# Writing out the order of attention half by half, in a kernel that runs block-sparse attention beside a two-layer product

## The chip, the core and the metric

One core of a Trainium2 chip runs the whole program. Its engines have a queue each and take their instructions in order: TensorE (PE, with its weight loads as PEld), VectorE (DVE), ScalarE (ACT), GpSimd (POOL), and SyncE (SP), which here only starts transfers. The metric is the time of one execution on the device, in microseconds.

## What is computed

Block-sparse attention over 4 batches, 8 heads, 768 positions and 64 elements a head. Positions are cut into 24 blocks of 32. A query block sees its neighbours, the first and the last block, and three sampled blocks; the first and the last query block see everything. Then two products with an exact Gelu between.

```python
mask = np.abs(blk_i - blk_j) <= window            # window = 1
mask = mask | (blk_i == 0) | (blk_j == 0) | (blk_i == n_blocks - 1) | (blk_j == n_blocks - 1)
for qb in range(n_blocks):
    for kb in sampled_blocks[qb]:                 # 3 of 24
        mask[qb * block:(qb + 1) * block, kb * block:(kb + 1) * block] = True
scores = np.where(mask, scale * q @ k.T, -1e9)
attn = softmax(scores) @ v                        # (4, 8, 768, 64)
...
x = attn.transpose(0, 2, 1, 3).reshape(3072, 512)
h = x @ w_in                                      # 512 -> 2048
g = 0.5 * h * (1.0 + erf(h / sqrt(2)))
out = g @ w_out                                   # 2048 -> 512
```

## The kernel before

**Units and stages.** The work is cut into eight units: half a batch each, 384 positions, three tiles ("quads") of 128. Units 0, 2, 4, 6 are the dense halves: they hold the two end blocks too, which see all 24 blocks. Units 1, 3, 5, 7 hold inner blocks alone. The loop at line 728 goes over units; in step n it issues the first products of unit n (`ffn1_step`, 64 matmuls, Gelu on ACT), and then the second products of unit n as 48 "pieces" (`ffn2_pieces`, one matmul each, 16 to an output tile), mixed into the attention of unit n+1. The pieces keep PE at work while DVE and ACT do the softmax. The first attention (unit 0) has idle products in their place, and the last second products stand alone (`last_output`).

**Rounds and groups.** A dense unit has four dense rounds `("d", x, G)`: one end block x (first or last) with one half G of the heads. All units have sparse rounds `("s", blocks)` of one or two query blocks; two sparse rounds, or one group of three blocks, make a group of up to 128 rows. In order, a round goes through `scores` (PE), `maxima` (DVE), `exponentials` (ACT) and `turned` (a transpose on DVE); a group goes through `values` (PE, in two halves), `divided` (DVE), and `outputs` (PE transposes, then an ACT copy into `xT`, which the next first products read). Where a unit of inner blocks is followed by a dense one, two rounds of the latter are done ahead (`ahead`).

**Buffers.** Scores take one of two buffers of `psA`, which is free again when the round's exponentials are done, and which the first products use as well. Values use `psV` (the last group of some units `psA`). Two banks change roles (`roles`): one holds the output tile of the pieces, the other takes the transposes of `outputs` and of `turn_pair`; they swap as a new output tile begins. So an output tile that is finished must be copied out by `store` (an ACT copy, line 532, then a transfer by SP) before the next transposes can use its bank. `ffn2_pieces` puts a finished tile in the list `finished`, and `store_finished` issues its copy wherever it is called: at the start of each new tile, and in `attention`.

**Order.** Nothing reorders the program: it stands in each engine's queue as the Python code issues it. Before, `attention` runs a loop over rounds. Each turn issues the scores of the next round, a division, a transpose, the maxima, the exponentials, a number of pieces from the list `quota`, an output, and value halves when `due`. `hooks` and `behind` put other work at given turns.

**Stage 0** has most of that: the keys and queries of batch 1 are turned on PE there, pair by pair (`turn_pair`, k0 to k3 and q0 to q3), each into the free bank and from there by a copy on ACT or DVE. `later_values` makes POOL read one element of turned query pair 2 (`hold_loads`), and then starts the eight loads of batch 1's values. In stage 1, DVE copies blocks into `gb` for unit 2 (`gather`, 27 copies on line 305), which read these values; unit 2's first `maxima` stands behind them in DVE's queue.

Of the kernel before, what the change touches and what calls it, by code (L numbers as in the profile page):

```python
# [10 lines left out]
F32 = mybir.dt.float32  # L11
# [9 lines left out]
def kernel(  # L21
# [10 lines left out]
    nc = tc.nc  # L32
# [213 lines left out]
    def turn_pair(which, pr):  # L246

        pt = turning_bank([P, PI, PP], "pt")
        turn_heads(which, pr, pt)
        dve = pr == 1  # L250
        if which == "k":
            (nc.vector.tensor_scalar_mul if dve else nc.scalar.mul)(
                keys(1)[:, 0:NB, BL * pr:BL * pr + BL].rearrange("q n (a i) -> q n a i", i=PI),
                pt.rearrange("q i (n a) -> q n a i", n=NB), 1.0 / 8.0)
        else:
            (nc.vector.tensor_copy if dve else nc.scalar.copy)(
                qTs[1][:, :, pr, :].rearrange("q c (p i) -> q c p i", i=PI),
                pt.rearrange("q i (c p) -> q c p i", c=NC))
# [50 lines left out]
    class Unit:  # L309
        def __init__(self, b, quads, dense):  # L310
            self.b, self.quads, self.dense = b, quads, dense
            self.groups = [[j for j in range(4 * t, 4 * t + 4) if 0 < j < NB - 1] for t in quads]
            self.js = [j for grp in self.groups for j in grp]
            self.place = {j: i for i, j in enumerate(sorted(self.js))}
            if b == 0 and dense:

                self.place = {j: 6 * t + i for t, grp in enumerate(self.groups) for i, j in enumerate(grp)}
            self.rounds = [("d", x, G) for G in (0, 1) for x in (0, 1)] if dense else []
# [15 lines left out]

    st = {}

    def scores(unit, rnd):
        qT, kT = qTs[unit.b % 2], keys(unit.b) if unit is not units[0] else k0
        A = psA.tile([P, 1024], F32, name="sc", tag="A")

        def product(o, G, hh, j, rhs):
            r = (hh % 2) ^ G
            rows = slice(64 * r, 64 * r + 64)
            pr = 2 * G + hh // 2
            nc.tensor.matmul(o, lhsT=qT[rows, j // 4, pr, BL * (j % 4):BL * (j % 4) + BL],  # L345
                             rhs=rhs(rows, pr), start=True, stop=True)
        if rnd[0] == "s":
            A4 = A.rearrange("p (g j c) -> p g j c", g=2, j=2)
            for i, j in enumerate(rnd[1]):
                x = unit.place[j]  # L350
                for hh in range(4):
                    for G in range(2):
                        product(A4[32 * hh:32 * hh + 32, G, i, :].rearrange(
                            "p (a c k) -> p a c k", a=2, k=BL), G, hh, j,
                            lambda rows, pr: seen_keys(x, rows, pr))
        else:
            _, x, G = rnd
# [4 lines left out]
        st[rnd, "A"] = A  # L362

    def maxima(rnd):
        A = st[rnd, "A"]
# [216 lines left out]
    def attention(unit, filler, quota, tail, hooks=None, late=False, ahead=None, when=None, behind={}):  # L582

        early = unit in closing
        done = begun.pop(unit, 0)  # L590
        rounds = [(unit, rnd) for rnd in unit.rounds[done:]]
        due = [(e - done + 1 + half, grp, half) for e, grp in sorted(unit.ends.items()) for half in range(2)]
        if when:
            due = [(at,) + x[1:] for at, x in zip(when, due, strict=True)]
# [3 lines left out]
        n, hooks = len(rounds), hooks or {}  # L598
        weighed, given = [], []

        def fill(m):
            for _ in range(m):
                next(filler, None)

        def weigh(it):
            _, grp, half = due.pop(0)
            halves = (half,)
            if due and due[0][0] <= it and due[0][1] == grp:
                halves += due.pop(0)[2:]
            values(unit, grp, halves)  # L610
            if 1 in halves:
                weighed.append(grp)

        def divide():
            divided(weighed[0])
            given.append(weighed.pop(0))
        for it in range(-1, n):
            last = it + 1 == n
            if not last:
                scores(*rounds[it + 1])  # L620
            else:
                while due and due[0][0] <= it:
                    weigh(it)
            ready = len(given)
            if weighed and not last:
                divide()
            if weighed and last and not early:
                divide()
            if it >= 1:
                turned(rounds[it - 1][1])  # L630
            if not last:
                maxima(rounds[it + 1][1])
            if it >= 0:
                exponentials(rounds[it][1])
            if last and not ahead:
                table(AF.Gelu)
            store_finished()
            for f in hooks.get(it, ()):
                f()
            fill(quota[it + 1])  # L640
            if not late:
                store_finished()
            if ready:
                outputs(unit, given.pop(0))
            while not last and due and due[0][0] <= it:
                weigh(it)
            for f in behind.get(it, ()):
                f()
        turned(rounds[n - 1][1])
        if early:  # L650
            divide()
        for f in hooks.get(n, ()):
            f()
        for m in tail[:-2]:
            fill(m)
            weigh(-1)
        assert not due
        fill(tail[-2])
        while len(given) > (not weighed):
            outputs(unit, given.pop(0))  # L660
        if weighed:
            divide()
        fill(tail[-1])
        outputs(unit, given.pop(0), 2)
        if ahead:
            table(AF.Gelu)
        for _ in filler:
            pass
        store_finished()
# [48 lines left out]
    attention(units[0], idle_products(30), [0, 3, 1, 8, 3, 6, 1, 1, 1, 2, 0], (0, 0, 0, 4),  # L718
              when=(5, 6, 7, 7, 8, 8, 10, 11),
              hooks={0: [lambda: fixed(1)], 1: [lambda: fixed(2, nc.scalar.copy, 0)],  # L720
                     3: [lambda: fixed(2, nc.scalar.copy, 1)], 4: [values_of(0)],
                     6: [values_of(1)], 8: [values_of(2)], 10: [more_numbers(J1[:3])]})

    def next_keys(b):
        place_keys(b)
# [2 lines left out]
    for n, unit in enumerate(units):  # L728
# [41 lines left out]
        if nxt is None:  # L770
            last_output(n)
        elif fresh:
            attention(nxt, filler, [1, 9, 4, 4, 4, 5, 3, 8, 3], (0, 0, 1, 4),
                      when=(2, 3, 4, 5, 6, 6, 8, 9))
        elif b + 1 < B:
            quota, tail, hooks, behind = [3, 10, 5, 4, 3, 8, 1, 5, 1], (0, 6), {}, {}
            if n == 0:
                quota, tail = [3, 11, 2, 3, 3, 6, 3, 4, 2], (0, 5)

                def later_values():  # L780
                    hold_loads(qTs[1][0:1, 0, 2, 0:1])
                    load_values(1)

                def pair(which, pr, pieces=0):
                    return [partial(next, filler, None)] * pieces + [partial(turn_pair, which, pr)]
                hooks = {1: pair("k", 0), 2: pair("k", 1, 2), 3: pair("q", 0, 1), 4: pair("k", 2, 2),
                         5: [later_values], 6: pair("q", 3), 8: [partial(spare_key, keys(1))]}
                behind = {3: pair("q", 1), 4: pair("q", 2), 5: pair("k", 3)}
            attention(nxt, filler, quota, tail, ahead=units[n + 2], hooks=hooks, behind=behind)
        else:  # L790
            attention(nxt, filler, [5, 8, 5, 5, 3, 8, 4], (0, 0, 1, 5),
                      when=(2, 3, 4, 4, 6, 7))


# [28 lines left out]
```

## Time and profile before

| what | us |
|---|---|
| median of three runs (lowest, highest) | 281.38 (281.14, 282.98) |
| the profiled execution | 284.88 |
| its span, first to last instruction | 283.1 |
| PE busy in the span | 253.0 |
| DVE, ACT, POOL busy | 206.3, 207.7, 101.7 |
| opening and unit 0's attention, to the first of the first products | 41.7 |
| last second products and the end | 13.7 |

A row of the order of time gives start, length, engine and line, operation, what it writes and reads with its size, how often it came in a row, and in brackets the idle time of the engine before it with what ended that. Waits on buffers show there. The mean granted clock of TensorE was 0.986.

### The profile page before, as it was taken

What the parts mean: (1) busy time and instruction counts of PE and PEld (TensorE: products, weight loads), DVE (VectorE), ACT (ScalarE), POOL (GpSimd) and SP (SyncE); (2) the same over time, 40 slices, a digit from 0 to 9 for tenths busy, and PEclk for the clock granted to TensorE, in tenths of its full rate; (3) what the DMA queues carried; (4) which work ended last, traced back from release to release, by engine and by line L of the source; (5) the groups of instructions that cost most, each with busy time, mean ns of one, the idle gap of its engine ahead of it and who ended that gap; (6) DMA issues with size and microseconds to landing.
All of it is one profiled execution on the core that took longest, in us unless ns stands there. A gap on an engine that the chain in (4) does not pass through costs nothing.

```text
span 283.1 us, 11427 instructions
## 1 busy us (share of the span) xinstructions
PE 253.0 (89%) x4860; PEld 143.6 (51%) x4918; DVE 206.3 (73%) x475; ACT 207.7 (73%) x380; POOL 101.7 (36%) x209
## 2 busy tenths in 40 slices
PE   1787669999898989999999899999999999999995
PEld 1623445455554455545564555445544566356644
DVE  7599839386779998688998878698948988782000
ACT  8779825896777885699668876896778866995611
POOL 8788950701897000580595000930040005000000
PEclk9999959999999999999999999999999999999999
DMA  6997299931999512991399218991101020021002
GB/s 101 175 89 124 40 195 202 206 73 40 95 156 145 132 41 73 122 99 51 23 153 171 71 42 132 95 75 43 41 0 39 8 76 0 0 80 39 2 37 75
DMA packets 72981, 23.80 MB, mean 84 GB/s; under 512 B 63073, under 2 KB 69474, under 8 KB 72930
## 3 DMA queue, kind: packets, MB, share of 16 engines
q0 software_dynamic: 56912, 13.64, 81.5%
q1 hardware_dynamic: 16018, 9.44, 12.9%
q8 instruction: 38, 0.62, 0.9%
q14 instruction: 13, 0.11, 0.1%
HBM read 27.26 MB, written 6.29 MB: 119 GB/s over the span
## 4 chain that ended last, share of the span: by engine, by line
PE 70%; DVE 12%; issue 6%; ACT 5%; DMA 4%; POOL 1%; DVEq 0%; POOLq 0%; ACTq 0%
PE hp L522 26%; PE op L548 20%; PE av L468 9%; PE sc L345 5%; DMA qn<-in_q_dram 4%; DVE nm L370 4%; DVE pT L404 2%; PE tx L497 2%; ACT pp L387 2%; PE op L578 2%; PE av L431 2%; DVE gb L305 2%; DVE nm L373 2%; PE pt L234 1%; PE av L578 1%
## 5 line engine op out<-in xcount | busy, mean ns | idle before, releaser
L522 PE MATMUL hp<-xT,w_in_sb 128*128 128x384 bf16 x512 | 85.1, 328 | 0.6 <-ACT xT L505 0.6
L387 ACT ACTIVATE pp<-sc,nm 128x256 bf16<-128x256 f32 x176 | 75.1, 544 | 9.4 <-DVE nm L370 9.1
L548 PE MATMUL op<-w_out_sb,g 128*128 128x512 bf16 x285 | 73.3, 380 | 6.3 <-issue 6.0
L522 PEld LDWEIGHTS <-w_in_sb 128*128 128x128 bf16 x512 | 50.3, 98 | 35.6 <-issue 3.0
L527 ACT ACTIVATE g<-hp 128x768 bf16<-128x768 f32 x56 | 45.2, 809 | 27.3 <-PE hp L522 27.3
L370 DVE TENSOR_REDUCE nm<-sc 128x4 f32<-128x1024 f32 (+1 forms) x48 | 52.8, 1106 | 7.9 <-PE sc L345 7.8
L305 POOL COPY gb<-kv 128x388 bf16 (+1 forms) x87 | 36.6, 474 | 24.8 <-DVE gb L296 22.9
L548 PEld LDWEIGHTS <-g 128*128 128x128 bf16 x336 | 27.7, 98 | 34.6 <-issue 10.4
L305 DVE COPY gb<-kv 128x388 bf16 x177 | 39.4, 300 | 1.9 <-DMA qn<-in_q_dram 1.9
L404 DVE STREAM_TRANSPOSE pT<-pp 128x512 f32<-128x512 f32 (+1 forms) x48 | 31.5, 656 | 6.6 <-ACT pp L387 6.4
L468 PEld LDWEIGHTS <-pT 64*32 64x32 bf16 (+1 forms) x2400 | 26.5, 92 | 18.0 <-issue 6.8
L468 PE MATMUL av<-kv,pT 64*32 64x130 bf16 (+1 forms) x1344 | 29.7, 223 | 3.9 <-issue 2.4
L165 POOL COPY mark<-gb 1x1 bf16<-1x1 bf16 x6 | 1.1, 179 | 79.7 <-DVE gb L305 79.7
L505 ACT COPY xT<-tx 128x512 bf16<-128x512 bf16 (+1 forms) x32 | 13.5, 448 | 13.7 <-PE tx L497 13.7
L141 POOL DMA_DIRECT2D kv<-in_v_dram x32 | 22.8, 721 | 1.8 <-DMA qn<-in_q_dram 1.1
L345 PE MATMUL sc<-gb,qT 64*32 64x256 bf16 x704 | 19.3, 274 | 3.6 <-ACT pp L391 1.5
L391 ACT ACTIVATE pp<-sc,nm 128x768 bf16<-128x768 f32 x16 | 17.2, 1107 | 5.9 <-DVE nm L373 5.9
L468 PE MATMUL av<-gb,pT 64*32 64x130 bf16 x1056 | 20.0, 224 | 0.0
L345 PEld LDWEIGHTS <-qT 64*32 64x32 bf16 x832 | 10.2, 90 | 19.1 <-issue 15.1
L415 ACT ACT_TABLE_LOAD x15 | 19.2, 1283 | 0.2
L487 DVE TENSOR_TENSOR xh<-av,rec 128x512 bf16<-128x512 f32 (+2 forms) x28 | 18.2, 652 | 1.0
L373 DVE TENSOR_REDUCE nm<-sc 128x1 f32<-128x768 f32 x16 | 14.7, 940 | 5.2 <-PE sc L345 4.9
(79 smaller groups left out, 232.8 us busy)
## 6 DMA issues: line engine op xcount, KB each, us to landing
out_dram<-os SPq DMA_DIRECT2D x23, 256.0 KB, 2.4
kv<-in_v_dram POOLq DMA_DIRECT2D x32, 96.0 KB, 6.6
w_out_sb<-in_moe_w_out_dram POOLq DMA_DIRECT2D x2, 1024.0 KB, 13.4
kn<-in_k_dram POOLq DMA_DIRECT2D x4, 384.0 KB, 11.3
qn<-in_q_dram POOLq DMA_DIRECT2D x4, 384.0 KB, 12.8
qn<-in_q_dram POOLq DMA_DIRECT2D x12, 128.0 KB, 5.4
kn<-in_k_dram POOLq DMA_DIRECT2D x12, 128.0 KB, 5.4
w_in_sb<-in_moe_w_in_dram POOLq DMA_DIRECT2D x2, 512.0 KB, 9.8
```

What stands on the lines that cost most here:

```text
L141: nc.gpsimd.dma_start(out=kvs[b % 2][32 * hh:32 * hh + 32, 0:NB, c0:c0 + D], in_=v[b, h].rearrange("(n p) d -> p n d", p=BL))
L305: (engine or nc.vector).tensor_copy(sampled(unit.place[j], r)[:, None, c0:c1], src[:, bass.ds(at[j][r], 1), :])
L345: nc.tensor.matmul(o, lhsT=qT[rows, j // 4, pr, BL * (j % 4):BL * (j % 4) + BL], rhs=rhs(rows, pr), start=True, stop=True)
L370: nc.vector.tensor_reduce(out=nm[:, 0:2 * n].rearrange("p (g j) -> p g j", g=2), in_=A4[:, :, 0:n, :], op=ALU.max, axis=AX.X, negate=True)
L373: nc.vector.tensor_reduce(out=nm[:, 0:1], in_=A[:, 0:S], op=ALU.max, axis=AX.X, negate=True)
L387: nc.scalar.activation(at[:, x // n, x % n], A[:, a:a + 256].rearrange("p (e c k) -> p e c k", e=2, k=BL), AF.Exp, bias=nm[:, x:x + 1])
L404: nc.vector.transpose(pt.rearrange("p g c x -> p (g c) x")[:, :, 64 * s:64 * (s + n)].bitcast(F32), pp[:, 0:512 * n].bitcast(F32).rearrang ...
L415: nc.scalar.activation(junk, zero[0:1, 0:1], func)
L468: nc.tensor.matmul(av[32 * s:32 * (s + w), h, V2 * G:V2 * G + V2], lhsT=pv[rows, G, c % 4, BL * s:BL * (s + w), c // 4], rhs=src[rows], st ...
L522: nc.tensor.matmul(hp[:, i, 0:T], lhsT=w_in_sb[:, ki, (m + i) * P:(m + i + 1) * P], rhs=xTs[n % 2][:, ki, 0:T], start=(ki == 0), stop=(ki ...
L527: nc.scalar.activation(g[:, m:m + 2, 0:T], hp[:, :, 0:T], AF.Gelu)
L548: nc.tensor.matmul(op, lhsT=g[:, m, t * P:(t + 1) * P], rhs=w_out_sb[:, m, :], start=(m == 0), stop=(m == KOUT - 1))
```

## The change

`attention` no longer works out its order from counts. It gets a plan, one word a step: `s` scores of a round (`s0+1`: two dense rounds in one, their matmuls alternating), `m` maxima, `e` exponentials, `t` turned, `f9` nine pieces, `w` values of group d, a, b or c (`wd0`, `wd1`: a half alone), `d` divided, `o` and `O` outputs, `x` other work, `G` the Gelu table. The text of the plans differs from the old order in these places:

- Values come whole, both halves together, but for unit 0's dense group.
- Pieces stand in fewer, longer runs.
- In stages 2 to 5 the dense rounds go in pairs: `s6+7` (rounds done ahead) and `s0+1`. To allow it, dense rounds of all batches but the second run over heads first, then end blocks.
- `store_finished` is called behind `e` steps alone (and, as before, at the start of a new tile and at the end); the calls behind each run of pieces are gone.
- In stage 0, `xq2`, `xv` (the hold and the value loads), `xk3` and `xq3` come behind the values of the last group. DVE copies k1, q2 and q3, where it copied k1 and q1.
- In stage 0 the spare key's copy stands at the end.

```diff
-        dve = pr == 1
+        dve = (which, pr) in (("k", 1), ("q", 2), ("q", 3))
...
+            order = [(x, G) for G in (0, 1) for x in (0, 1)] if b == 1 else [(x, G) for x in (0, 1) for G in (0, 1)]
+            self.rounds = [("d", x, G) for x, G in order] if dense else []
...
-    def scores(unit, rnd):
+    def scores(unit, *rnds):
...
             for c0, c1 in ((0, 512), (512, 768)):
                 for hh in range(4):
-                    product(A[32 * hh:32 * hh + 32, c0:c1], G, hh, (NB - 1) * x,
-                            lambda rows, pr: kT[rows, c0 // BL:c1 // BL, BL * pr:BL * pr + BL])
+                    for A, (_, x, G) in zip(tiles, rnds):
+                        product(A[32 * hh:32 * hh + 32, c0:c1], G, hh, (NB - 1) * x,
+                                lambda rows, pr: kT[rows, c0 // BL:c1 // BL, BL * pr:BL * pr + BL])
...
+    def attention(unit, filler, plan, extra={}, ahead=None):
...
+        for word in plan.split():
+            what, arg = word[0], word[1:]
...
+            if what in "met":
+                {"m": maxima, "e": exponentials, "t": turned}[what](rounds[int(arg)][1])
+                if what == "e":
+                    store_finished()
...
-            attention(nxt, filler, [1, 9, 4, 4, 4, 5, 3, 8, 3], (0, 0, 1, 4),
-                      when=(2, 3, 4, 5, 6, 6, 8, 9))
+            attention(nxt, filler,
+                      ("s0 m0 f1 s1 m1 e0 f9 " if b == 0 else "s0+1 m0 m1 e0 f11 ") + "s2 t0 m2 e1 f4 s3 t1 m3 e2 f3 wd s4 t2 dd m4 e3 f10 s5 t3 m5 e4 wa s6 t4 m6 "
+                      "e5 f6 od f5 s7 da t5 m7 e6 wb t6 e7 G f3 oa t7 db wc f1 ob dc f3 Oc")
+        elif n == 0:
...
+            attention(nxt, filler,
+                      "s0 m0 f3 s1 m1 e0 f11 s2 t0 m2 e1 xk0 f2 s3 t1 m3 e2 f2 xk1 f2 wa s4 t2 m4 e3 da f1 xq0 e4 f5 "
+                      "xq1 f1 s5 t3 m5 wb s6 e5 t4 db t5 m6 oa f1 xk2 f3 s7 wc e6 m7 e7 dc f2 ob t6 f2 xq2 xv f3 xk3 "
+                      "t7 f4 xq3 f3 Oc xs G", extra | {"v": later_values, "s": partial(spare_key, keys(1))},
+                      ahead=units[n + 2])
         elif b + 1 < B:
-            quota, tail, hooks, behind = [3, 10, 5, 4, 3, 8, 1, 5, 1], (0, 6), {}, {}
-            if n == 0:
-                quota, tail = [3, 11, 2, 3, 3, 6, 3, 4, 2], (0, 5)
...
+            attention(nxt, filler,
+                      "s0 m0 f3 s1 m1 e0 f9 s2 t0 m2 e1 f5 s3 t1 m3 e2 f3 wa s4 t2 m4 e3 da e4 f11 oa f1 s5 t3 m5 wb "
+                      "e5 t4 db t5 s6+7 f2 ob m6 e6 m7 f1 wc e7 dc t6 f7 t7 f3 Oc G", ahead=units[n + 2])
+        else:
+            attention(nxt, filler,
+                      "s0 m0 f5 s1 m1 e0 f7 s2 t0 m2 e1 f5 s3 t1 m3 e2 f3 wa s4 t2 m4 e3 da e4 f11 oa f1 s5 t3 m5 wb "
+                      "e5 G t4 t5 db f2 wc dc f3 ob f6 Oc")
```

For comparison, the order of stage 0 before, in the same words: `s0 m0 f3 s1 m1 e0 f11 s2 t0 m2 e1 xk0 f2 s3 t1 m3 e2 f2 xk1 f3 wa0 s4 t2 m4 e3 f1 xq0 f3 wa1 xq1 s5 da t3 m5 e4 f2 xk2 f6 wb0 xq2 s6 t4 m6 e5 xv f3 oa wb1 xk3 s7 db t5 m7 e6 xq3 f4 wc dc t6 e7 f2 ob t7 xs f5 Oc G`.

More of the change, by code (lines that the diff above doesn't have):

```diff
@@ L335 @@
     st = {}
-    def scores(unit, rnd):
+    def scores(unit, *rnds):
         qT, kT = qTs[unit.b % 2], keys(unit.b) if unit is not units[0] else k0
-        A = psA.tile([P, 1024], F32, name="sc", tag="A")
+        tiles = [psA.tile([P, 1024], F32, name="sc", tag="A") for _ in rnds]
         def product(o, G, hh, j, rhs):
@@ L580, in last_output @@
             store(n, quad, cols, op)
-    def attention(unit, filler, quota, tail, hooks=None, late=False, ahead=None, when=None, behind={}):
-        early = unit in closing
+    def attention(unit, filler, plan, extra={}, ahead=None):
         done = begun.pop(unit, 0)
         rounds = [(unit, rnd) for rnd in unit.rounds[done:]]
-        due = [(e - done + 1 + half, grp, half) for e, grp in sorted(unit.ends.items()) for half in range(2)]
-        if when:
-            due = [(at,) + x[1:] for at, x in zip(when, due, strict=True)]
         if ahead:
@@ L597, in attention @@
             rounds += [(ahead, rnd) for rnd in ahead.rounds[0:AHEAD]]
[L598 to L635, printed above, removed]
-                table(AF.Gelu)
[L637 to L666, printed above, removed]
+        groups = dict(zip("dabc" if unit.dense else "abc", [grp for _, grp in sorted(unit.ends.items())], strict=True))
@@ L717, in more_numbers @@
         return load
[L718 to L722, printed above, removed]
+    attention(units[0], idle_products(30),
[3 rows of a table added]
+              {"f1": lambda: fixed(1), "f2": lambda: fixed(2, nc.scalar.copy, 0),
+               "f3": lambda: fixed(2, nc.scalar.copy, 1), "v0": values_of(0), "v1": values_of(1),
+               "v2": values_of(2), "n": more_numbers(J1[:3])})
     def next_keys(b):
```

54 lines of the change are left out of this document (37 added, 17 removed), and 3 rows, old and new, of the table js.

## The prediction

> **What bounds the kernel now.** I read the page's head, then the busy times by stretch, then the order of time inside one stage of each kind. "Stage n" is the first products of unit n (64 matmuls of line 522), then its second products (48 pieces of line 548) mixed with the attention of unit n+1.
>
> ```profile
> span 283.1 us, 11427 instructions
> PE 253.0 (89%) x4860; PEld 143.6 (51%) x4918; DVE 206.3 (73%) x475; ACT 207.7 (73%) x380; POOL 101.7 (36%) x209
> ```
>
> ```profile
> 53.50:76.90 23.40, 21.29 (x569) 12.12 (x575) 17.39 (x28) 19.00 (x37) 7.97 (x21) 1.00 1.05 87
> 89.00:109.60 20.60, 18.49 (x539) 10.37 (x545) 17.77 (x35) 16.09 (x36) 2.89 (x7) 1.00 0.54 80
> 120.60:138.80 18.20, 17.25 (x442) 8.88 (x448) 15.97 (x26) 15.27 (x33) 6.54 (x14) 1.00 1.61 58
> 149.80:170.20 20.40, 18.82 (x547) 10.46 (x555) 17.44 (x32) 16.76 (x37) 2.89 (x7) 1.00 0.65 90
> ```
>
> The columns are the stretch, its length, and the busy time of PE, PEld, DVE, ACT and POOL. These are the attention parts of stages 0, 1, 2 and 3. PE is short of the whole by 2.1, 2.1, 1.0 and 1.6 us, and part of that is hand-over between groups. So PE's in-order queue sets the time of a stage. What an edit is worth is the matmul time that it takes out, less the new places where PE meets a buffer or a tile that isn't ready.
>
> **What PE's work costs.** Starts of groups in stage 2 give the price from one start to the next:
>
> ```profile
> 121.13 0.41 PE L345 MATMUL sc<-gb,qT 64*32 64x256 bf16 x16
> ...
> 123.76 0.41 PE L345 MATMUL sc<-gb,qT 64*32 64x256 bf16 x16
> ...
> 125.30 0.41 PE L345 MATMUL sc<-gb,qT 64*32 64x256 bf16 x16
> ...
> 129.16 0.30 PE L345 MATMUL sc<-gb,qT 64*32 64x256 bf16 x8
> ...
> 131.23 0.58 PE L468 MATMUL av<-kv,pT 64*128 64x130 bf16 x28
> ...
> 131.84 0.54 PE L345 MATMUL sc<-kv,qT 64*32 64x512 bf16 x8
> ...
> 133.47 0.54 PE L345 MATMUL sc<-kv,qT 64*32 64x512 bf16 x8
> ...
> 135.12 0.55 PE L468 MATMUL av<-kv,pT 64*32 64x130 bf16 x24
> ...
> 136.47 0.39 PE L497 MATMUL tx<-identity,xh 128*128 128x128 bf16 x4 [0.16 <-issue]
> ```
>
> Ten pieces and a 16-matmul score take 2.63 us, five and one take 1.54: a piece is 0.218, the score 0.45. Eight pieces and an 8-matmul score take 2.07, so that score is 0.33. A dense round (8 matmuls, 3072 columns) with five pieces takes 1.65, so it is 0.56. A values half takes 0.61 (131.23 to 131.84), the three-block group with one piece 1.35, so 1.13 alone.
>
> **Paired dense rounds** (`s0+1`, `s6+7`: four pairs, in stages 2 to 5). The 16-matmul score alternates both row halves inside each column group, and its second 2048 columns cost 0.12 us, 0.059 ns a column. A lone dense round has 0.56 - 0.21 = 0.35 us for 3072 columns, 0.114 ns each. If the pair, which alternates the row halves in the same way, reaches the better rate, it costs 0.21 + 6144 x 0.059 = 0.57 instead of 1.12. Bounds: it saves 0 or 0.55 a pair; I take 0.55, the rate of the same tile shape in the same alternation.
> The Trainium skill (TensorE: Matmul & The Clock Gate, Measured speedup vs the span model) puts a pack at one matmul's duration plus about 4 ns a tile; as an estimate that makes the pair 0.32 us cheaper, and the sum below 0.9 us worse. No run here shows a pair.
>
> **Stage 0** keeps all its instructions, with three turned pairs (k1, q2, q3) copied by DVE where it was k1 and q1. What moves is the copy that stores a finished output (line 532): it was also placed behind each run of pieces, now only behind a round's exponentials.
>
> ```profile
> 57.15 0.53 PE L234 MATMUL pt<-identity,kn 96*64 96x96 bf16 x16
> ...
> 57.95 0.77 ACT L252 ACTIVATE kv<-pt 128x768 bf16<-128x768 bf16 x1
> ...
> 58.63 0.57 ACT L532 COPY os<-op 128x512 f32<-128x512 f32 x1
> ...
> 59.10 3.29 ACT L387 ACTIVATE pp<-sc,nm 128x256 bf16<-128x256 f32 x8
> ...
> 59.30 0.53 PE L234 MATMUL pt<-identity,kn 96*64 96x96 bf16 x16
> ...
> 64.39 0.96 DVE L256 COPY qT<-pt 128x768 bf16<-128x768 bf16 x1 [1.56 <-PE pt L234]
> ...
> 65.40 0.53 PE L234 MATMUL pt<-identity,kn 96*64 96x96 bf16 x16 [0.31 <-DVE qT L256]
> ...
> 72.17 0.53 PE L234 MATMUL pt<-identity,qn 96*64 96x96 bf16 x16 [0.46 <-ACT kv L252]
> 72.17 0.92 DVE L373 TENSOR_REDUCE nm<-sc 128x1 f32<-128x768 f32 x1
> ...
> 73.66 1.15 ACT L391 ACTIVATE pp<-sc,nm 128x768 bf16<-128x768 f32 x1
> ```
>
> (a) The second turn (k1, PE at 59.30) starts right as the store at 58.63 ends, since it takes that bank. In the changed order four exponentials (e2, half of 3.29 = 1.65 us) stand ahead of the store on ACT. PE waits at k1: +1.6.
> (b) The second output's last piece falls into "dc f2", behind `e7`. Its store then follows s7 0.56, m7 0.92, e7 1.1, itself 0.58, with hand-overs 3.3 us; PE has s7, wc 1.13 and f2, 2.1, to do until `ob` needs that bank: +1.2.
> (c) q2, k3, q3 and `Oc` now follow each other through one bank with 3 to 4 pieces (0.65 to 0.87) between, against a copy of 0.96 and its hand-overs; `oa` to k2 and t3 to wb are tight too. I sum 2.1 us of waits (0.2 wb, 0.5 k2, 0.3 q2, 0.5 k3, 0.1 q3, 0.5 Oc) against 0.8 in the two rows shown, and since part of them falls where PE waits for smaller things today, I take +1.0.
> Stage 0: +3.8; bounds 0, if every copy is done in time, and +5, if each of the four turns waits its copy out.
>
> **Stage 1: the value loads leave late.** This is the largest single term.
>
> ```profile
> 68.62 0.80 ACT L256 COPY qT<-pt 128x768 bf16<-128x768 bf16 x1 [0.88 <-PE pt L234]
> ...
> 69.48 0.18 POOL L165 COPY mark<-qT 1x1 bf16<-1x1 bf16 x1 [14.07 <-ACT qT L256]
> 69.71 5.63 POOL L141 DMA_DIRECT2D kv<-in_v_dram  x8
> ...
> 77.11 10.56 PE L522 MATMUL hp<-xT,w_in_sb 128*128 128x384 bf16 x64 [0.19 <-ACT xT L505]
> ...
> 82.23 7.31 DVE L305 COPY gb<-kv 128x388 bf16 x27 [1.86 <-DMA qn<-in_q_dram]
> ...
> 89.47 1.81 DVE L373 TENSOR_REDUCE nm<-sc 128x1 f32<-128x768 f32 x2
> ...
> 90.44 2.08 ACT L391 ACTIVATE pp<-sc,nm 128x768 bf16<-128x768 f32 x2 [0.73 <-DVE nm L373]
> ...
> 91.60 0.41 PE L345 MATMUL sc<-gb,qT 64*32 64x256 bf16 x16 [0.69 <-ACT pp L391]
> ```
>
> `hold_loads` on POOL waits for q2's copy, then eight loads go out, and DVE's 27 gathers wait for them: 12.8 us from mark (69.48) to first gather (82.23). Behind the gathers in DVE's queue stands the next unit's first maximum, behind that its exponentials, and s2 on PE needs that buffer. Let X be the start of the first products (77.11). The copy ends at X - 7.7, gathers start at X + 5.1, s2 at X + 14.5; PE is ready at X + 13.8. In the changed plan q2 stands behind wc and ob. After its transposes PE has only f3, k3, f4, q3, f3, Oc, f3 (13 pieces 2.8, two turns 0.94, 0.18 = 3.95) and waits of 1.1, while its own copy takes 1.0: it ends at X - 4.05. So gathers at X + 8.7, s2 at X + 18.2, and PE waits 4.5 instead of 0.7: +3.8. In the same stage the store of the second output lands behind e5, and `od` waits about 0.5 for its bank; a wait of 0.25 at s7 goes. Stage 1: +4.0. Bounds: -0.7 if the loads land as fast as the fastest of the eight (below), +5 if the query loads that follow at once slow them.
>
> **Stages 2 to 6.** The short rounds have these durations:
>
> ```profile
> 131.02 0.65 DVE L370 TENSOR_REDUCE nm<-sc 128x2 f32<-128x512 f32 x1
> ...
> 131.77 0.94 ACT L387 ACTIVATE pp<-sc,nm 128x256 bf16<-128x256 f32 x2
> ...
> 134.78 0.43 DVE L404 STREAM_TRANSPOSE pT<-pp 128x256 f32<-128x256 f32 x1
> ```
>
> Stages 2 and 4: the pair saves 0.55, but it needs both score buffers, so it waits for e5: s5 0.33, m5 0.65, e5 0.94, hand-overs 0.15 against s5 and wb (two halves, 1.22): 0.5 lost. That leaves about -0.1 each (from -0.55, if e5 is early, to +0.5, if the pair doesn't pack). Stages 3 and 5: pair -0.55, `od` behind the store +0.5, s7's wait -0.25, but s0 waits for one more Gelu +0.15: -0.1 each. Stage 6 has no pair: wc stands one f2 behind wb and needs t5 (s5, m5, e5, t5 and hand-overs 2.55 against s5, wb, f2 2.0), +0.5, and s2 with one piece less ahead of it +0.2: +0.7. In the opening unit only rounds of equal shape swap: 0. DVE's table of copies and all DMA counts stay, so nothing else is priced.
>
> **Sum.** 3.8 + 4.0 - 0.2 - 0.2 + 0.7 = +8.1 on a span of 283.1. That profiled execution took 284.88 with what lies around it, the runs' median is 281.38; scaled by their ratio (0.988) the sum is 8.0. The forecast is 281.4 + 8.0 = 289.4 us.
>
> **Rivals.**
> 1. *The waits hide one another* (0.13). Stage 0's PE waits are taken up and only the order counts: q2 comes 2.7 us of PE work later than now, its copy ends at X - 4.9, and s2 waits 3.5, +2.8. With +0.3 from the later stages the total is +3.1: 284.5. For it: ACT and DVE have 4 to 6 us free in stage 0. Against: PE runs its queue in order, so a wait at k1 moves everything behind it.
> 2. *The loads land earlier* (0.07).
>
> ```profile
> L141 POOL DMA_DIRECT2D kv<-in_v_dram x8: 709/709/721, 69.7 to 74.6; - x8
> ...
> DMA to landing us min/median/max: 3.0/6.1/7.2
> ```
>
> With the shortest landing, 3.0, the last load would be in 8.1 us after the mark; then s2 waits for nothing, stage 1 gives -0.5, the sum is 3.8 - 0.5 + 0.3 = 3.6: 285.0. Against it: the last gather's wait ended 7.6 after the last issue.
> The Trainium skill (DMA: Bandwidth & Descriptors, Anatomy of one DMA) fits a load at 2.0 us plus bytes over 436 GB/s, 2.2 us for 96 KB, an estimate that would give this rival; the trace's median of 6.1 us speaks against it, and the measurement decides.
> 3. *Not slower* (0.07). The mechanism is PE's matmul count alone: four pairs save 2.2 us, and it decides if the three banks are released before PE asks for them and the gathers are in before X + 12. For it, PE is 89% busy. Against: both releases are in ACT's and POOL's queues behind later work. It gives 281.4 - 2.2 = 279.2 us.
> 4. *Pairs don't pack, or the query loads delay the values* (0.09): +2.2 or +1 more, about 291.5.
>
> **How the numbers follow.** The forecast has 0.64, with its own range 286 to 291.5; the rivals have 0.13, 0.07, 0.07, 0.09. Leaving out rival 3 and half of rival 4, the range is 284.0 to 292.0. A measurement of this kernel can tell about 1% from no change. Faster by over 1% (below 278.6) needs more than rival 3 gives at its middle: 0.03. Within 1% (to 284.2) take the rest of rival 3 and a third of rivals 1 and 2: 0.11. Slower: 0.86.
>
> **What would show it.** In stage 0, k1's transposes start behind a store that stands after e2, at 60.9 instead of 59.3; `ob` waits for a store; the first products start near 81. POOL's mark comes near 76.5, the gathers near 89.3, and s2 of stage 1 waits over 4 us for ACT. Stages 2 and 4 stay within 0.5 us of 18.2; the pairs take under 0.7 us. I am wrong if the gathers start before 86, or if stage 0 is under 25.5 us.

## The result and the profile after

The changed kernel takes 292.36 us (median of 4 runs, 290.81 to 294.27) against 281.81 for the kernel before beside it: a ratio of 1.037 (1.030 to 1.045), 10.5 us slower. The forecast was 289.4 with a range up to 292.0: the direction and the places were right, the change was put at 8.0 us instead of 10.5, and the time lies 0.4 us above the range.

The head of the page of the changed kernel, its slices of PE and of the granted clock:

```profile
span 292.4 us, 11479 instructions
PE 262.3 (90%) x4918; PEld 142.7 (49%) x4918; DVE 207.2 (71%) x476; ACT 208.1 (71%) x379; POOL 101.2 (35%) x209
...
PE   1798799687995799999999999999999999999995
...
PEclk9999999999999599999999999999999999999999
```

PE's busy time is 9.3 us higher although no matmul was added, but most of that isn't real: the trace of before lacks 58 matmul records (weight loads are 4918 in both). The traces of e9 and e10 (below) have all 4918 and no slow clock, and show 260.5 and 259.7 us, so the rise is about 2 us. (The shortfalls of PE by stretch that the prediction read contain such missing records too.) The one 5 in the clock's row, 0.5 in the fourteenth slice (95 to 102 us), accounts for it: there a 16-matmul score and four pieces take 2.37 us from start to start (97.09 to 99.46), where they take 1.32 at full clock in E11.

The page of before has such a 5 too, in its sixth slice (35 to 42 us), behind a stop of PE in the opening:

```profile
PEclk9999959999999999999999999999999999999999
```

```profile
34.06 0.75 PE L468 MATMUL av<-kv,pT 64*32 64x130 bf16 x21
37.20 0.26 PE L468 MATMUL av<-kv,pT 64*32 64x130 bf16 x1 [2.39 <-issue]
```

The clock was at 0.50 from 36.3 to 43.1 us there. So the page that the forecast was made from already showed a gap of PE followed by a slow clock.

Stage by stage, from the first products of one unit to those of the next. The starts of the rows of line 525 (522 before) give the lengths in us; the column 7 ends at the third of the four groups of the last second products. E1 and e9 are explained below.

| | opening | 0 | 1 | 2 | 3 | 4 | 5 | 6 | 7 |
|---|---|---|---|---|---|---|---|---|---|
| before | 41.74 | 35.37 | 32.43 | 29.19 | 31.41 | 29.21 | 31.41 | 27.97 | 17.31 |
| after | 38.19 | 40.03 | 39.11 | 29.30 | 31.44 | 29.33 | 31.36 | 29.33 | 17.31 |
| e1, after with an early hold | 37.62 | 39.52 | 31.53 | 29.29 | 31.43 | 29.33 | 31.37 | 29.21 | 17.30 |
| e9, before with an early hold | 37.66 | 35.72 | 31.43 | 29.18 | 31.42 | 29.22 | 31.41 | 27.98 | 17.31 |

The loss is in stages 0 (+4.7), 1 (+6.7) and 6 (+1.4). One trap: the profiled execution of before took 284.88 us, more than the four that are timed (281.14 to 282.98), with an opening of 41.7 us where the others here have 37.6 to 38.7; that of after is the slowest of its four. So absolute times of the two traces differ by 3.55 us before stage 0 begins, and positions are compared from the start of their stage.

The longest waits of PE in stages 0 and 1 of the changed kernel (total, count, longest):

```profile
PE sc L347 <- ACT pp L394: 5.1, 1, 5.1
PE tx L500 <- ACT os L535: 1.7, 2, 1.3
PE pt L234 <- ACT os L535: 1.4, 1, 1.4
PE pt L234 <- DVE den L486: 1.2, 1, 1.2
PE op L551 <- DMA w_out_sb<-in_moe_w_out_dram: 0.7, 1, 0.7
PE pt L234 <- ACT xT L508: 0.7, 2, 0.5
```

And the same in order of time on PE:

```profile
57.49 0.53 PE L234 MATMUL pt<-identity,kn 96*64 96x96 bf16 x16 [1.44 <-ACT os L535]
...
61.79 0.53 PE L234 MATMUL pt<-identity,qn 96*64 96x96 bf16 x16 [1.19 <-DVE den L486]
...
71.75 0.39 PE L500 MATMUL tx<-identity,xh 128*128 128x128 bf16 x4 [1.25 <-ACT os L535]
...
72.81 0.53 PE L234 MATMUL pt<-identity,qn 96*64 96x96 bf16 x16 [0.24 <-ACT xT L508]
...
74.39 0.53 PE L234 MATMUL pt<-identity,kn 96*64 96x96 bf16 x16 [0.30 <-DVE qT L256]
...
77.40 0.33 PE L500 MATMUL tx<-identity,xh 96*128 96x96 bf16 x4 [0.30 <-DVE qT L256]
...
97.09 0.63 PE L347 MATMUL sc<-gb,qT 64*32 64x256 bf16 x16 [5.06 <-ACT pp L394]
```

Both new waits on the store (`os`) are there, at k1 and at `ob`, and s2 of stage 1 waits 5.06 us for the exponentials behind the gathers. The other two engines of that chain show why. (The row of the gathers names a query load as what ended their wait. Releasers are inferred. The gathers copy out of `kv`; the last of its eight loads goes out at 79.6 us and the slowest takes 8.1 us to land, which makes 87.7, just ahead of the gathers; E1 supports it.)

```profile
74.40 0.18 POOL L165 COPY mark<-qT 1x1 bf16<-1x1 bf16 x1 [21.53 <-DVE qT L256]
74.64 5.75 POOL L141 DMA_DIRECT2D kv<-in_v_dram  x8
```

```profile
88.48 6.54 DVE L305 COPY gb<-kv 128x388 bf16 x27 [7.74 <-DMA qn<-in_q_dram]
94.95 1.81 DVE L376 TENSOR_REDUCE nm<-sc 128x1 f32<-128x768 f32 x2
```

What the prediction lacked stands in the busy times by stretch (length; busy time of PE, PEld, DVE, ACT and POOL; granted clock; share of the transfer engines and GB/s):

```profile
94.00:95.00 1.00, 0.00 (x0) 0.00 (x0) 1.00 (x8) 0.00 (x0) 0.00 (x0) 1.00 2.60 153
95.00:96.00 1.00, 0.00 (x0) 0.00 (x0) 1.00 (x3) 0.07 (x1) 0.84 (x3) 0.88 2.47 164
96.00:97.00 1.00, 0.00 (x0) 0.00 (x0) 0.76 (x1) 1.00 (x2) 1.00 (x3) 0.50 2.41 121
97.00:101.00 4.00, 3.91 (x39) 1.02 (x38) 3.12 (x4) 2.73 (x6) 1.05 (x3) 0.50 0.76 166
101.00:105.00 4.00, 4.00 (x120) 2.67 (x119) 2.38 (x6) 2.22 (x5) 0.00 (x0) 0.80 0.19 70
```

PE stops at 92.03. After nearly four idle microseconds the granted clock falls to 0.50, and PE resumes at half speed: the 16-matmul score at 97.09 is busy for 0.63 us where those at full clock take 0.41. The mean of 0.80 in the last row puts the return to 1.0 at about 102.6. The Trainium skill (TensorE: Matmul & The Clock Gate, HAM oscillation — how this bites in real kernels) tells its reader to leave no PE gap longer than about 3.4 us for this reason. The trace agrees for this gap: 5.06 us of waiting were followed by about 5.5 us of work at 0.50. But the traces of this case show that a gap under 3.4 us isn't safe either, and there the measurement decides. The 2.39 us in before and 2.96 us in E2 were followed by 0.50 as well, and so was a wait of 1.42 us at k1 in E5, after which the turn takes 0.85 us instead of 0.53:

```profile
56.57 0.85 PE L234 MATMUL pt<-identity,kn 96*64 96x96 bf16 x16 [1.42 <-ACT os L535]
```

The same wait of 1.44 or 1.45 us in after, E1, E3 and E10 was not. Each time the low clock lasted for either 3.41 us (E2, E4, E5) or 6.83 us (before, after, E7), and the longer gap doesn't always get the longer time: 2.39 us got 6.83, the 4.31 us of E4 got 3.41.

### The profile page after: what moved, and what is told of

The parts are those of the page before. It is cut to its first block, busy times and chain, and to the rows that moved or that the text cites. A ratio compares the mean times of both kernels' runs of the same rounds, so it can differ in the third digit from the quotient of the medians.

```text
span 292.4 us, 11479 instructions
## 1 busy us (share of the span) xinstructions
PE 262.3 (90%) x4918; PEld 142.7 (49%) x4918; DVE 207.2 (71%) x476; ACT 208.1 (71%) x379; POOL 101.2 (35%) x209
## 3 DMA queue, kind: packets, MB, share of 16 engines
q1 hardware_dynamic: 16018, 9.44, 12.8%
## 4 chain that ended last, share of the span: by engine, by line
PE 55%; DMA 14%; ACT 12%; DVE 7%; POOL 7%; issue 3%; POOLq 1%; DVEq 0%; ACTq 0%
PE hp L525 21%; PE op L551 16%; DMA kn<-in_k_dram 6%; PE av L471 5%; DMA qn<-in_q_dram 5%; ACT pp L390 5%; PE sc L347 4%; DMA kv<-in_v_dram 3%; ACT L418 3%; POOL gb L305 3%; DVE nm L373 3%; PE tx L500 2%; PE op L581 2%; POOL kv L141 2%; PE av L434 2%
## 5 line engine op out<-in xcount | busy, mean ns | idle before, releaser
L551 PE MATMUL op<-w_out_sb,g 128*128 128x512 bf16 x336 | 87.4, 386 | 0.8 <-DMA w_out_sb<-in_moe_w_out_dram 0.7
L373 DVE TENSOR_REDUCE nm<-sc 128x4 f32<-128x1024 f32 (+1 forms) x48 | 53.5, 1119 | 13.8 <-PE sc L347 13.2
L551 PEld LDWEIGHTS <-g 128*128 128x128 bf16 x336 | 28.3, 98 | 34.5 <-issue 10.4
L305 DVE COPY gb<-kv 128x388 bf16 x177 | 37.9, 293 | 7.8 <-DMA qn<-in_q_dram 7.7
L471 PE MATMUL av<-kv,pT 64*32 64x130 bf16 (+1 forms) x1344 | 30.8, 221 | 3.1 <-issue 1.5
L471 PEld LDWEIGHTS <-pT 64*32 64x32 bf16 (+1 forms) x2400 | 25.4, 91 | 11.8 <-DVE pT L407 3.5
L347 PEld LDWEIGHTS <-qT 64*32 64x32 bf16 x832 | 9.2, 90 | 28.0 <-issue 21.9
L418 ACT ACT_TABLE_LOAD x15 | 19.2, 1283 | 0.2
```

The costliest lines, as they stand in the source:

```text
L305: (engine or nc.vector).tensor_copy(sampled(unit.place[j], r)[:, None, c0:c1], src[:, bass.ds(at[j][r], 1), :])
L373: nc.vector.tensor_reduce(out=nm[:, 0:2 * n].rearrange("p (g j) -> p g j", g=2), in_=A4[:, :, 0:n, :], op=ALU.max, axis=AX.X, negate=True)
L418: nc.scalar.activation(junk, zero[0:1, 0:1], func)
L471: nc.tensor.matmul(av[32 * s:32 * (s + w), h, V2 * G:V2 * G + V2], lhsT=pv[rows, G, c % 4, BL * s:BL * (s + w), c // 4], rhs=src[rows], st ...
L551: nc.tensor.matmul(op, lhsT=g[:, m, t * P:(t + 1) * P], rhs=w_out_sb[:, m, :], start=(m == 0), stop=(m == KOUT - 1))
```

## The experiments

My theory after the first look: stage 1 loses its wait and the clock behind it because the loads leave late; stage 0 loses by the store that now stands behind exponentials and by turns crowded in one bank; stage 6 by its new order; the pairs give next to nothing. The runs below try these.

**E1: the hold reads an earlier query pair.** In the changed kernel:

```
-                hold_loads(qTs[1][0:1, 0, 2, 0:1])
+                hold_loads(qTs[1][0:1, 0, 1, 0:1])
```

> The changed kernel with one index edited: POOL's hold ahead of batch 1's value loads reads turned query pair 1 instead of pair 2, so the loads may start some 9 us earlier (pair 1's copy ended at 65.5 us in the changed kernel's profile, pair 2's at 74.3). Theory (the late loads cost stage 1 a wait of 5.1 us and, behind it, some 2.5 us of half clock): the 7.7 us wait of DVE's gathers goes, s2 of stage 1 starts within 15 us of the first products (19 now), the clock stays at 1.0, and the time falls by 6 to 7 us, to about 286. Rival (stage 1 is long for its own new order, and the wait would move elsewhere): the gathers start early but the time falls by less than 4.

Measured: 285.48 us (ratio 1.014, 1.011 to 1.017), 6.9 us less than the changed kernel. POOL's queue:

```profile
64.46 0.18 POOL L165 COPY mark<-qT 1x1 bf16<-1x1 bf16 x1 [12.12 <-ACT qT L256]
64.69 5.65 POOL L141 DMA_DIRECT2D kv<-in_v_dram  x8
```

The mark is 10 us earlier, s2 of stage 1 has no wait, the mean clock is 1.0 and stage 1 is 31.53 us. So all of stage 1's loss hangs on when the value loads leave.

**E2: a late hold in the kernel before.** There the hold reads pair 3 instead of pair 2.

> The kernel before with one index edited: the hold reads query pair 3 instead of pair 2, whose copy ended 4.3 us later (73.8 against 69.4 us). Nothing else of the change is in it. Theory: gathers start at about 86.6 instead of 82.2, s2 of stage 1 at 96 instead of 91.6 (+4.4), PE is idle some 5 us before it, the granted clock falls to 0.5 for about 5 us, which costs another 2 to 2.5: +6.5 us in all, 288.3. Rival (the low clock of the changed kernel has another cause than the idle time): +4.4, 286.2, clock at 1.0.

Measured: 285.02 us (1.011, 1.007 to 1.016), by another way than expected: I had overlooked that `later_values` stands ahead of the last pair's turn in that kernel. The hold met a tile that nothing had written yet, and the loads left early:

```profile
52.48 0.18 POOL L165 COPY mark<-qT 1x1 bf16<-1x1 bf16 x1
52.60 4.25 POOL L141 DMA_DIRECT2D kv<-in_v_dram  x6
```

Stage 1 is 31.42 here, and stage 0 is 40.17, longer by over 4 us (35.72 in E9). PE's queue shows most of it in one gap, in the middle of a values half, with no wait that the profile shows:

```profile
59.59 0.22 PE L468 MATMUL av<-gb,pT 64*32 64x130 bf16 x4
62.77 0.42 PE L468 MATMUL av<-gb,pT 64*32 64x130 bf16 x20 [2.96 <-issue]
```

Behind the gap the granted clock is 0.50 from 62.9 to 66.3 us, which makes up the rest. So this run says nothing on late loads. It says that loads can also leave too early. What PE waits for in the gap isn't shown: the 8 loads and the last key and query loads are in flight, and that PE's own instructions come late beside them is a guess that no run tried.

**E3: the gap filled with useless matmuls.** The changed kernel computes 20 products more ahead of s2 of stage 1, which nothing reads:

```
+        for _ in range(20):
+            nc.tensor.matmul(T, lhsT=identity, rhs=w_out_sb[:, 0, :], start=True, stop=True)
```

> The changed kernel with 20 matmuls more, of no use, on PE in stage 1 between the nine pieces and s2, where PE was idle for 5.1 us: 20 x 0.216 = 4.3 us of work in that gap, into the bank that is free there. Theory (half clock because of the idle time): s2 starts no later, the clock stays at 1.0 in the 5.5 us behind it, and the kernel gets 2 to 2.7 us faster though it does more work: about 290. Rival (the clock falls for another reason, such as the transfers then in flight): no gain, 292.4, and the clock still at 0.5.

Measured: 292.46 us (1.040, 1.036 to 1.045). Stage 1 fell from 39.11 to 36.10 with the clock at 1.00 throughout, as the theory had it: from s2 to the next first products it took 17.97 us instead of 20.24, so the clock cost 2.27 us. Counted from the start of the stage, s2 also came 0.7 us earlier (18.1 instead of 18.9). But the median didn't move: stages 2, 4 and 6 grew to 29.82, 29.79 and 30.24, and in stage 6 PE stops for 1.32 us ahead of nothing but its own issue. E12 takes that up.

**E4: the store behind each run of pieces again**, in the changed kernel:

```
                 for _ in range(int(arg)):
                     next(filler, None)
+                store_finished()
                 continue
```

> The changed kernel with the copies of finished output tiles issued behind each run of pieces too, as before the change. Theory (PE met a bank whose store stood behind exponentials on ACT): the waits for ACT's store go, 1.4 us at k1 and 1.25 at ob in stage 0, and 0.5 at od in each of stages 1, 3 and 5; q2 in stage 0 comes 2.5 us earlier, the value loads too. Stage 0 loses 2 to 2.7 us, stage 1 between 0.5 and 1, stages 3 and 5 0.3 to 0.5 each: 288.5, between 287.5 and 289.5. Rival (other waits take their place in stage 0, ACT's exponentials come later): less than 1.5 us gained.

Measured: 292.54 us (1.041, 1.036 to 1.046): the expectation missed. In the trace stage 0 went from 40.03 to 38.27 and the wait for the store at k1 is gone. These waits of PE remain in that stretch, the one for `os` at `ob`:

```profile
PE pt L234 <- DVE rec L488: 1.6, 1, 1.6
PE tx L500 <- ACT os L535: 1.3, 1, 1.3
PE pt L234 <- ACT xT L508: 0.9, 2, 0.7
```

`ob` still waits, since the piece that ends the output comes only after e7, so no place of the store call helps it; the 0.5 us at `od` in stage 1 stayed too. The wait at q0 grew from 1.19 to 1.65. The trace has stage 1 shorter as well (37.26 instead of 39.11, s2 waiting 4.31 us), since the clock was low for 3.41 us here and for 6.83 in after. That is no gain of the edit: both kernels have one execution with a mean clock of 0.994, 290.63 and 290.81 us, and three at 0.987 or 0.988, 292.0 to 294.3 and 292.3 to 294.3. At the same clock the times agree within their own spread. So k1's wait is shown to come from the store's place, but it is worth nothing in the total that these runs can show.

**E5: E1 with the paired rounds one after the other** instead of alternating:

```
-                scores(rounds[at[0]][0], *[rounds[i][1] for i in at])
+                for i in at:
+                    scores(rounds[i][0], rounds[i][1])
```

> The changed kernel with the early hold (pair 1, as in the run before), and with the paired dense rounds issued one after the other at the same places (s0 then s1, s6 then s7); all else as there. Compared with the early hold alone (285.5 us). Theory (a pair packs: 0.56 instead of 1.1 us): stages 2 to 5 are 0.4 to 0.55 us longer each, 1.6 to 2.2 in all: 287.3. Rival (the time of a pair is set by its waits, e5 for s6+7 and Gelu for s0+1, so that splitting them lets the first round start earlier): less than 0.8 in all, 286.2 or below.

Measured: 285.76 us (1.012, 1.007 to 1.017) against 285.48 of e1, no difference. The start of stage 3 in e1, and then in e5:

```profile
148.46 0.56 PE L347 MATMUL sc<-kv,qT 64*32 64x512 bf16 x16
149.18 2.32 PE L551 MATMUL op<-w_out_sb,g 128*128 128x512 bf16 x10 [0.16 <-issue]
151.61 0.41 PE L347 MATMUL sc<-gb,qT 64*32 64x256 bf16 x16
```

```profile
148.64 0.56 PE L347 MATMUL sc<-kv,qT 64*32 64x512 bf16 x16
149.35 2.32 PE L551 MATMUL op<-w_out_sb,g 128*128 128x512 bf16 x10 [0.16 <-issue]
151.80 0.41 PE L347 MATMUL sc<-gb,qT 64*32 64x256 bf16 x16
```

To the next score it is 3.15 and 3.16 us, with 11 pieces (2.40), one of which has no record: the two rounds cost 0.75 in either order of their matmuls. Before, a piece stands between them, which has no record either:

```profile
149.22 0.51 PE L345 MATMUL sc<-kv,qT 64*32 64x512 bf16 x8
149.98 0.50 PE L345 MATMUL sc<-kv,qT 64*32 64x512 bf16 x8 [0.25 <-ACT g L525]
150.41 2.12 PE L548 MATMUL op<-w_out_sb,g 128*128 128x512 bf16 x9
152.46 0.41 PE L345 MATMUL sc<-gb,qT 64*32 64x256 bf16 x16
```

That is 3.24 with 10 pieces (2.18), 1.06 for the two. So standing next to each other saves 0.3 us, the alternation nothing.

**E6: E1 with the old order of stage 0**: the old plan of that attention, its table of copies and its store calls.

```
-        dve = (which, pr) in (("k", 1), ("q", 2), ("q", 3))
+        dve = pr == 1
...
-  "... e2 f2 xk1 f2 wa s4 ... f2 xq2 xv f3 xk3 t7 f4 xq3 f3 Oc xs G"
+  "... e2 f2 xk1 f3 wa0 s4 ... f2 xk2 f6 wb0 xq2 ... xv f3 oa wb1 xk3 s7 ... xq3 f4 ... Oc G"
```

> The changed kernel with the early hold, and with the order of stage 0 as before the change (its copies on ACT and DVE too, and stores behind each run of pieces); the new order stands in all other stages. Compared with the early hold alone (285.5). Theory (the order of stage 0 costs its PE waits at k1, ob, k2, q2, k3, Oc): stage 0 gets 3.5 us shorter and nothing else changes: 282.0, with an excess over the kernel before that is stage 6's 1.3 less 0.9 from the wait at s2 that the early hold removes. Rival (stage 0 is paced by the transfers and by PE's own code, not by this order): less than 2 us gained.

Measured: 281.85 us (1.000, 0.997 to 1.002; 10 runs), 3.6 less than e1, stage 0 at 35.19. The store calls come back in every stage by this edit, but stages 1 to 6 stay within 0.3 us of e1. So the new order of stage 0 costs 3.6 us as a whole.

**E7: the kernel before with its loads behind the last query pair.**

```
-                         5: [later_values], 6: pair("q", 3), 8: [partial(spare_key, keys(1))]}
+                         6: pair("q", 3) + [later_values], 8: [partial(spare_key, keys(1))]}
```

The hold reads pair 3, which now is written ahead of it.

> The kernel before with the hold and the value loads moved behind the turn of query pair 3, and the hold reading that pair, so that it really waits for it (in the run with the late hold above it was read before it was written, and the loads left at 52.5 us). Pair 3's copy ended 4.3 us after pair 2's. Theory (late loads alone): gathers start 4.3 us later, PE is idle for about 5 us ahead of s2 of stage 1, the granted clock falls to 0.5 for some 5 us behind it: +4.3 + 2.3 = +6.6, 288. Rival (idle without the clock): +4.3, 285.8, with the clock at 1.0 throughout.

Measured: 288.12 us (1.019, 1.013 to 1.025). With nothing else of the change in it, stage 1 becomes 39.74 instead of 32.43, and the same rows appear: a long wait, then a slow clock.

```profile
92.98 0.63 PE L345 MATMUL sc<-gb,qT 64*32 64x256 bf16 x16 [5.57 <-ACT pp L391]
```

```profile
93.00:99.00 6.00, 5.67 (x94) 2.32 (x95) 4.09 (x5) 4.62 (x10) 0.94 (x3) 0.53 0.58 144
```

**E8: the changed kernel's code with the old orders written as its plans**, E1's hold, and the pair kept at the start of stages 3 and 5 alone.

> All orders as before the change, written as plans, with stores behind each run of pieces; of the change only the pair s0+1 in stages 3 and 5 is kept (with the order of dense rounds that it needs), and the early hold is added. Theory (the pair saves PE time where PE is the bound, and the hold takes away the 0.7 us that s2 of stage 1 waits): stages 3 and 5 get 0.5 shorter each, stage 1 0.7 to 0.9: 279.6, faster than both kernels. Rival (a pair's gain is lost to the waits behind it, DVE being as late): only the hold's gain, 280.6.

Measured: 280.26 us (0.994, 0.992 to 0.996; 10 runs): better than both kernels, by 1.5 us against the one before. Stage 1 is 31.42, stages 3 and 5 31.33 and 31.31.

**E9: the kernel before with the early hold alone**, the edit of E1.

> The kernel before, with one edit: the loads of the later values wait for the second query pair's copy instead of the third's. Theory: the mark leaves about 4 us earlier, s2 of stage 1 waits for nothing, stage 1 goes from 32.4 to 31.4 us and the whole from 281.8 to 280.8; then the early hold is all that the combined kernel (0.994 of before) gained but 0.2. Rival: the pairs and the plan's other small changes carry part of that gain, and the early hold alone stays within 0.5 us of before (281.3 or more).

Measured: 280.44 us (0.996, 0.994 to 0.998; 12 runs). The mark is at 61.68, and stage 1 31.43: this one index gives 1.1 of E8's 1.5 us. The order written out is not needed for it; the pairs' 0.1 a stage is in E8's trace, and the two medians can't show it.

**E10: E1 with the old order of stage 6 alone.**

```
-  "... wa s4 t2 m4 e3 da e4 f11 oa f1 s5 t3 m5 wb e5 G t4 t5 db f2 wc dc f3 ob f6 Oc"
+  "... wa0 s4 t2 m4 e3 f3 wa1 s5 da t3 m5 e4 f8 wb t4 e5 G f4 oa t5 db wc f1 ob dc f5 Oc"
```

> The changed kernel with the early hold and the old order of the last attention (stage 6) alone. Theory: the new order of stage 6 costs 1.3 us, so stage 6 goes from 29.2 to 28.0 and the whole from 285.5 (early hold alone) to 284.2. Rival: what stage 6 lost hangs on the state in which the stage before leaves the buffers, and stage 6 stays above 28.8.

Measured: 284.50 us (1.010, 1.006 to 1.013), 1.0 less than e1; stage 6 27.98 again. So the loss of stage 6 is in its own order. In the changed kernel most of it shows in the three-block group `wc`:

```profile
262.48 0.24 PE L471 MATMUL av<-kv,pT 64*32 64x130 bf16 x4
262.96 0.30 PE L471 MATMUL av<-kv,pT 64*32 64x130 bf16 x12 [0.24 <-DVE den L486]
263.81 0.29 PE L471 MATMUL av<-kv,pT 64*32 64x130 bf16 x8 [0.54 <-issue]
```

It begins while t5 is being transposed on DVE (262.46 to 262.91), waits for it, and then stops once more with nothing shown. That last gap varies with the run, 0.54, 0.40, 0.77 and 0.26 in after, e1, e5 and e6, and stage 6 varies by the same: 29.33, 29.21, 29.55, 29.04. Without the gap it is 28.8 in all four, 0.8 above the old order.

**E11: E7 with the 20 useless matmuls in its gap.**

> The kernel before with its later values loaded behind the last query pair's turn (which alone gave 288.1 us), and 20 useless matmuls ahead of s2 in stage 1, in the gap where PE waited 5.6 us. Theory of the clock: PE stays busy, the granted clock stays at 1.0, stage 1 goes from 39.7 to about 37 and the whole from 288.1 to 285.6, since this kernel's later stages keep their old order. Rival: the clock in that gap costs little and the useless matmuls only fill time, stage 1 stays above 38.8.

Measured: 287.74 us (1.020, 1.017 to 1.024). The wait ends at the same place as in E7, s2 at 92.88 (19.25 us into the stage, 19.37 there), but now the clock holds:

```profile
93.00:99.00 6.00, 5.98 (x173) 2.99 (x164) 5.32 (x8) 5.19 (x12) 0.85 (x2) 1.00 0.77 165
```

The stretch has 173 matmul records where E7's has 94, and stage 1 is 36.96 instead of 39.74. From s2 to the next first products it is 17.71 us instead of 20.37: the clock cost 2.66 us. The total again gained less, since stages 2 and 4 grew by 0.85 each, with one stop of PE marked "issue" in either, 0.58 and 0.61 us.

**E12: E9 with the same 20 matmuls**, where there is no gap to fill.

> The kernel before with the early hold (280.4 us alone) and the same 20 useless matmuls ahead of s2 in stage 1, where here there is no gap to fill. Theory: the 0.6 to 0.85 us by which stages 2 and 4 grew in both kernels with the 20 matmuls comes from the 20 extra instructions themselves, which move all later ones in PE's instruction stream; then stages 2 and 4 are about 30.0 here too, stage 1 is 20 x 0.217 = 4.3 us longer (35.8), and the whole is 280.4 + 4.3 + 1.6 = 286.3. Rival: the growth belongs to the late loads or the filled gap; stages 2 and 4 stay at 29.2 and the whole comes to 284.8.

Measured: 286.25 us (1.017, 1.014 to 1.020); the total is as the theory had it. Stage 1 is longer by 4.3 us, and stages 2 to 4 by 0.3, 0.1 and 1.0, where 0.8 was expected in 2 and 4, with gaps in the middle of groups like this one:

```profile
190.58 0.23 PE L468 MATMUL av<-gb,pT 64*32 64x130 bf16 x1 [0.79 <-issue]
```

So the 20 extra instructions cost 1.4 us in later stages without any late load or gap. Growth of this size, 1.9 us in the trace of E3 and 1.7 in that of E11, explains most of why the clock's gain doesn't show in their totals. Whether it is the place of the later instructions in PE's stream, as I think, or another effect of the added work, these runs don't tell.

## Why the prediction was short

By medians, the experiments add up to the whole. The early hold is worth 6.9 in the changed kernel and 1.1 in the old one (E1, E9: 281.56 to 280.44), so stage 1 lost 5.8 through the change. Stage 0's order cost 3.6 (E6), stage 6's 1.0 (E10). Together 10.4, of 10.5 measured. Counted against the kernel before as it ran beside each run, the split is 5.4, 3.9 and 1.1, so a part is known to 0.4 us. The forecast had 4.0, 3.8 and 0.7, and -0.4 for the stages between.

1. **Stage 1, forecast +4.0, measured +5.4 to +5.8 (6.7 in the trace): the mis-sized term, and the failed step.** The chain was right. Counted from X, the start of the first products (78.22), the mark comes at X - 3.8 (the copy ahead of it was forecast to end at X - 4.05), the gathers start at X + 10.3 (+8.7) and take 6.5 us (7.3 before), and s2 stands at X + 18.9 (+18.2) after 5.06 us (4.5). What failed is "PE waits 4.5 instead of 0.7: +3.8": I priced a wait of that length at its length alone. In the trace it is 4.4 us more of waiting, and then work at half clock that costs 2.27. E3 and E11 took the slow clock away, with s2 0.7 and 0.1 us earlier in its stage: from s2 on, 2.27 and 2.66 us. Adding 2.3 to the forecast gives 291.7. A PE gap above 4 us was forecast and its place was named; its consequence stood in the clock row of before, behind a gap of 2.39 us.
2. **The loads' landing.** From mark to first gather it was 14.1 us instead of the 12.8 carried over, and the gathers then ran faster, so s2 came only 0.7 later. The slowest landing of the eight was 8.1 us against 7.2. Rival 4's delay by the query loads fits that; no run tried it. Rival 2 is refuted: nothing landed early. (The 7.6 us that the prediction held against it is the first gather's wait, not the last's.)
3. **Stage 0, forecast +3.8, measured +3.6 to +3.9 (E6): right.** (a) Forecast k1 at 60.9, 19.2 us into the stage; it is at 19.3, with 1.44 us of wait behind the store. (b) `ob` 1.2, measured 1.25. (c) The turns: forecast 1.0 more than the 0.8 of before, measured 0.46, 0.24, 0.30 and 0.30 at k2, q2, k3 and Oc, 1.3 in all, and 1.19 at q0, which I hadn't named. The cause of that one stays open: the releaser shown differs between runs, and it isn't always an engine. That the parts' sum fits is thus partly luck, and so is that +3.8 met 3.6: without q0, (c) would be 0.5.
4. **Pairs, forecast 0.55 each: wrong in size and cause.** They give 0.3 us, by standing next to each other; alternation gives nothing (E5). Of my two bounds the truth lay between. They are not "under 0.7 us", as I had said they would show: 0.75, and 1.05 for the busy time of the pair in stage 2, which can't end before e5 does (141.14, the pair runs from 140.66). The net for stages 2 to 5 stayed within 0.15 us a stage, since the small gain was taken by that wait and by `od` behind its store (0.5 measured and forecast).
5. **Stage 6, forecast +0.7, measured +1.0 (1.4 in the trace).** The wait for t5 was right. The gap behind it, 0.3 to 0.8, was not in the sum.
6. **The base.** I took the profiled execution of before as it stood and scaled the sum by 0.988. Its extra 3.5 us lay in the opening, in the gap of 2.39 us and the half clock behind it, so the scaling did no good, though it cost only 0.1. "First products near 81" and "gathers near 89.3" carried that opening with them; the trace has 78.2 and 88.5 with an opening 3.55 shorter.

## What to carry to other kernels

A forecast wait of the matmul engine can have a second price: all five waits of 2.39 us or more that the traces show past the first 20 us were followed by a low clock, and one of eight of 1.3 to 1.65 us. Add the half-speed work behind it, or shorten the wait. A hold that spaces out loads should read the earliest tile that gives the spacing needed, and when an order is rewritten, every such hold moves with the tile it reads: here one index was worth 6.9 us in the changed kernel, while the only gain found in the new order was 0.3 a pair. When a trace of before has an outlying opening, compare by stage and not by time since the start, and ask what made it long.

## What was not expected of the hardware

- Waits of 5.06 and 5.57 us on PE were followed by a granted clock of 0.50 for some 5 us of work, at 2.3 to 2.7 us a time (after, E7; E3 and E11 without it). So were gaps of 4.31 (E4), 2.96 (E2), 2.39 (before) and once 1.42 us (E5), and the low clock lasted 3.41 or 6.83 us each time.
- PE stops in the middle of a group with no wait that the profile shows: 2.39 us in before, 2.96 in E2, 0.26 to 0.77 in `wc`, 0.79 in E12.
- 20 matmuls that nothing reads cost 4.3 us where they stand and 1.4 us in later stages (E12).
- Loads can leave too late (E7, +6.4 us) and too early (E2, +3.6), within 18 us of one another: the marks were at 70.32 and 52.48, and the best of those tried at 61.68 (E9).
